# Five instead of eight transfers outstanding on SyncE's queue, in a fused attention and gated-linear-unit kernel

## The chip, the cores and the metric

The kernel runs on one core of a Trainium2 chip. The core has five engines with instruction streams of their own: TensorE (PE, with its weight loads shown as PEld), VectorE (DVE), ScalarE (ACT), GpSimd (POOL) and SyncE (SP), and 16 DMA engines that move data between HBM and the on-chip memory. SyncE computes nothing here: it issues transfers. The metric is the time of one execution on the device, in microseconds (us).

## The reference

Blockwise causal attention over 8 batches, 8 heads, 576 positions and 64 features is followed by a gated linear unit whose gate comes from a causal convolution over five positions:

```python
def _attn_ref(q, k, v):
    block = 64
    scores = scale * np.matmul(q, k.transpose(0, 1, 3, 2))
    mask = block_i >= block_j          # by blocks of 64 positions
    scores = np.where(mask, scores, -1000000000.0)
    scores = scores - np.max(scores, axis=-1, keepdims=True)
    attn = np.exp(scores)
    attn = attn / (np.sum(attn, axis=-1, keepdims=True) + 1e-09)
    return np.matmul(attn, v)

def _moe_ref(x, w_val, conv_w, w_out):   # x: heads side by side, (8, 576, 512)
    for k in range(5):
        gate_pre += conv_w[k] * xp[:, k:k + S, :]
    gate = 1.0 / (1.0 + np.exp(-gate_pre))
    return gate * (x @ w_val) @ w_out
```

All inputs and the output are float32.

## The kernel before

The order of all work is written out by hand: `PLAN` (lines 12 to 118) is a list of words such as `lv/9.0/S`, each an operation, its arguments, the engine and, for TensorE, the PSUM banks. A loop at the end of the kernel (line 677) calls the operations in that order, so each engine's instruction order is the order of its words. Semaphores between engines are put in by the framework, from what each instruction reads and writes.

The work is cut by heads. A unit u (16 of them) is four heads, half a batch; a pair p (32 of them) is two heads. For each unit, q and k are loaded in two halves each (`lq`, `lk`, line 272, 288 KB a half) into the float32 tiles `qs` and `ks`, of which there are three each. A cast to float16 (`cd`) goes into `qk16`, TensorE transposes it (`Tt`), a copy (`Te`) brings it into `qkT`, and TensorE makes the scores (`S`), ScalarE the exponentials (`E`). For each pair, v is loaded in two halves (`lv`, line 285, 128 KB each) into `vs`, five tiles, and cast (`cv`) into `v16`; the last 64 positions of v of a whole batch come separately (`lvt`, line 291, tile `vts`, cast `cvt`, used by the products `AT`). The products with v (`A`) are normalized and transposed into `xt`. Over runs of 464 positions follow the convolution (`C`), its gate (`CS`), the value product (`V`) and the gating (`Ve`), and then, per 128 rows, the output product (`O`), its copy (`Oe`) to one of six tiles `osb`, and the store (`Od`, line 649, 256 KB). The two weight matrices come in two transfers each (`lwv` line 296, `lwo` line 301) and the convolution's weights in one (`lcv` line 306). Most casts are made by GpSimd, some by VectorE and ScalarE. In the first microseconds TensorE also runs products on a zero tile (`w0`).

All transfers but two are issued by SyncE, one after the other, in the order of the list. Only `OLd` (line 662), the two last stores of 128 KB, is issued by ScalarE. A transfer waits at SyncE until its buffer is free, or, for a store, until its data is there; while it waits, the transfers behind it in the list wait too. Each transfer reports its landing on one of eight semaphores, taken in turn. The transfer eight places later uses the same semaphore and waits for that landing before it is issued, so at most eight are outstanding at a time. The choice of the engine is this dictionary, and a transfer is issued like this:

```python
    DMA = {"S": nc.sync, "A": nc.scalar}
...
        DMA[eng].dma_start(out=rot(qks[i], u)[0:128, h], in_=x)
```

Of the kernel before, what the change touches and what calls it, by code (L numbers as in the profile page):

```python
# [121 lines left out]
def kernel(  # L122
# [16 lines left out]
    B, H, SEQ, D = q.shape  # L139
# [20 lines left out]
    def consts(n, shape, dt, tag):  # L160
        return [const(shape, dt, f"{tag}_{i}") for i in range(n)]
# [52 lines left out]
    olast = [late[0:128, 256 * i:256 * i + 256] for i in range(2)]  # L214
    conv_nat = late[0:5, 0:512]

    qks = [consts(3, [128, 2, 576], fp32, f"{n}s") for n in "qk"]
    vs = consts(5, [128, 4, 2, 64], fp32, "vs")
    vts = consts(2, [128, 8, 64], fp32, "vts")
# [14 lines left out]
    w_val_st = gv[0:128, 0:4096].bitcast(fp32).rearrange("p (f n) -> p f n", f=4)  # L234
    gv = gv.rearrange("p (f s) -> p f s", f=4)
    osb_all = const([128, 6 * 512], fp32, "osb")
    osb = [osb_all[0:128, 512 * i:512 * i + 512] for i in range(6)]
    w_out_st = osb_all[0:128, 0:2048].rearrange("p (f n) -> p f n", f=4)
# [5 lines left out]
    def rot(tiles, i):  # L244
        return tiles[i % len(tiles)]

    DMA = {"S": nc.sync, "A": nc.scalar}

    def copy(eng, out, in_):
        if eng == "A":  # L250
            i = nc.scalar.copy(out=out, in_=in_)  # L251
        else:
            i = (nc.vector if eng == "V" else nc.gpsimd).tensor_copy(out=out, in_=in_)  # L253
        made.append(i)
# [10 lines left out]
    def load_qk(i, u, h, eng):  # L265
        b, w = divmod(u, 2)
        x = (q, k)[i][b]
        if u in ALONE:
            x = x[4 * w + 2 * h:4 * w + 2 * h + 2].rearrange("y (p n) d -> (y p) (n d)", n=9)
        else:  # L270
            x = x[4 * w + h:4 * w + h + 3:2].rearrange("x (p n) d -> p x (n d)", n=9)
        DMA[eng].dma_start(out=rot(qks[i], u)[0:128, h], in_=x)  # L272

    @op
    def lq(u, h, eng="S", bank=None):
        load_qk(0, u, h, eng)

    @op
    def lk(u, h, eng="S", bank=None):
        load_qk(1, u, h, eng)  # L280

    @op
    def lv(p, h, eng="S", bank=None):
        b, g = divmod(p, 4)
        DMA[eng].dma_start(
            out=rot(vs, p)[0:128, 0:4, h, 0:64],
            in_=v[b, 2 * g + h, 0:512, 0:64].rearrange("(c p) d -> p c d", p=128))

    @op
    def lvt(b, eng="S", bank=None):  # L290
        DMA[eng].dma_start(out=vts[b % 2][0:64, 0:8, 0:64],
                           in_=v[b, 0:8, 512:576, 0:64].rearrange("h s d -> s h d"))

    @op
    def lwv(f, eng="S", bank=None):
        DMA[eng].dma_start(out=w_val_st[0:128, 2 * f:2 * f + 2],
                           in_=moe_w_val[256 * f:256 * f + 256].rearrange("(f p) n -> p f n", p=128))

    @op
    def lwo(f, eng="S", bank=None):  # L300
        DMA[eng].dma_start(out=w_out_st[0:128, 2 * f:2 * f + 2],
                           in_=moe_w_out[256 * f:256 * f + 256].rearrange("(f p) n -> p f n", p=128))

    @op
    def lcv(eng="S", bank=None):
        DMA[eng].dma_start(out=conv_nat[0:5, 0:512], in_=moe_conv_w[:, :])


    @op
# [325 lines left out]
    def rows(u, t):  # L635
        return out2d[1152 * u + 128 * t:1152 * u + 128 * t + 128]
# [9 lines left out]

    @op
    def Od(u, t, eng, bank=None):
        DMA[eng].dma_start(out=rows(u, t), in_=rot(osb, 9 * u + t)[0:128])

    @op
    def OL(i, eng, bank):
# [6 lines left out]

    @op  # L660
    def OLd(i, eng, bank=None):
        DMA[eng].dma_start(out=rows(B // 2 - 1, 8)[:, 256 * i:256 * i + 256], in_=olast[i][0:128])

    nc.vector.memset(wz[0:128], 0.0)
    nc.vector.memset(tiny[0:128], 0.0)  # L665
# [11 lines left out]
    for word in PLAN.split():  # L677
        name, args, eng, bank = (word.split("/") + [""])[0:4]
        a = [int(i) for i in args.split(".") if i]
# [51 lines left out]
```

## Time and profile before

| | |
|---|---|
| time, median of 3 runs | 176.22 us (175.95 to 177.16) |
| the profiled execution: time | 175.31 us |
| the profiled execution: span of the instructions | 173.5 us |
| mean granted TensorE clock | 0.997 |
| DMA | 40.37 MB, 53693 packets, mean 233 GB/s |
| HBM | 30.42 MB read, 9.44 MB written |

All times inside the kernel are counted from the start of the span. In the rows of the profile, a line begins with the kernel's line, the engine and the operation, then what it writes and reads, as in `vs<-in_v_dram` for a load of v. SPq is the sequencer of SyncE, where transfers are issued. A row of transfers gives their count, the size of one and the median time from issue to landing; a row with min/median/max in front of its times gives the three of them for a group. A row of waits names who waited for whom, the total in us, how often, and the longest. A row of the order of time gives start, duration, the instruction, and in brackets the idle time of the engine before it and what ended it. The engine groups that take most time are the products of TensorE (line 146), ScalarE's exponentials (line 424, 93.4 us) and VectorE's copies out of PSUM (line 253). Line 253 is the shared helper of copies and casts.

### The profile page before, as it was taken

What the parts mean: (1) busy time and instruction counts of PE and PEld (TensorE: products, weight loads), DVE (VectorE), ACT (ScalarE), POOL (GpSimd) and SP (SyncE); (2) the same over time, 40 slices, a digit from 0 to 9 for tenths busy, and PEclk for the clock granted to TensorE, in tenths of its full rate; (3) what the DMA queues carried; (4) which work ended last, traced back from release to release, by engine and by line L of the source; (5) the groups of instructions that cost most, each with busy time, mean ns of one, the idle gap of its engine ahead of it and who ended that gap; (6) DMA issues with size and microseconds to landing.
All of it is one profiled execution on the core that took longest, in us unless ns stands there. A gap on an engine that the chain in (4) does not pass through costs nothing.

```text
span 173.5 us, 7920 instructions
## 1 busy us (share of the span) xinstructions
PE 165.5 (95%) x3397; PEld 96.6 (56%) x3397; DVE 127.5 (73%) x256; ACT 138.0 (80%) x162; POOL 72.2 (42%) x144
## 2 busy tenths in 40 slices
PE   7889999999999999999999999999999999999991
PEld 2335566457554865675445657484656565665440
DVE  4377998389968889799339879998699895645420
ACT  4589999789958989988987785898989768853641
POOL 5222836846367763671356418160466112100000
PEclk9999999999999999999999999999999999999998
DMA  5999899999999998999988999899688010302565
GB/s 170 333 380 259 198 302 384 331 191 279 253 215 280 245 186 258 298 337 333 289 253 244 333 252 261 253 311 243 148 289 268 7 62 2 117 14 95 192 231 212
DMA packets 53693, 40.37 MB, mean 233 GB/s; under 512 B 39701, under 2 KB 39957, under 8 KB 53658
## 3 DMA queue, kind: packets, MB, share of 16 engines
q1 hardware_dynamic: 53370, 39.61, 78.0%
q8 instruction: 26, 0.43, 1.0%
q10 hardware_dynamic: 288, 0.26, 0.4%
q14 instruction: 9, 0.07, 0.2%
HBM read 30.42 MB, written 9.44 MB: 230 GB/s over the span
## 4 chain that ended last, share of the span: by engine, by line
PE 77%; DVE 11%; issue 4%; DMA 3%; ACT 2%; SPq 1%; POOL 0%; DVEq 0%; POOLq 0%
PE PS L146 70%; PE PS L150 7%; DVE qkT L253 5%; DMA ks<-in_k_dram 3%; DVE gv L624 2%; ACT pt L424 1%; DVE x L494 1%; DVE xt L253 1%; DVE v L253 1%; DVE rc L489 1%; SPq L272 0%; POOL k L253 0%; DVE DG L570 0%; ACT xt L251 0%; DVE late L253 0%
## 5 line engine op out<-in xcount | busy, mean ns | idle before, releaser
L424 ACT ACTIVATE pt<-PS 128x1024 f16<-128x1024 f32 x96 | 93.4, 1027 | 11.9 <-PE PS L146 10.8
L253 DVE COPY qkT<-PS 128x1152 f16<-128x1152 f16 (+1 forms) x27 | 34.7, 1287 | 10.2 <-PE PS L150 9.2
L624 DVE SCALAR_TENSOR_TENSOR gv<-th,PS 128x112 f16<-128x112 f32 (+5 forms) x64 | 25.8, 448 | 16.1 <-PE PS L146 8.5
L146 PE MATMUL PS<-w_out,gv 128*128 128x512 f16 (+1 forms) x148 | 35.7, 374 | 0.3
L146 PE MATMUL PS<-xt,w_val 128*128 128x464 f16 x160 | 35.8, 360 | 0.1
L146 PE MATMUL PS<-qkT 64*128 64x64 f16 (+4 forms) x384 | 34.5, 276 | 0.6 <-DVE qkT L253 0.5
L146 PEld LDWEIGHTS <-pt 128*128 128x128 f16 (+1 forms) x960 | 28.0, 102 | 7.6 <-issue 2.8
L146 PE MATMUL PS<-v,pt 128*128 128x65 f16 (+1 forms) x896 | 30.7, 194 | 0.5 <-DVE rc L489 0.4
L606 ACT ACTIVATE th<-PS 128x928 f32<-128x928 f32 x20 | 18.0, 945 | 8.2 <-PE PS L146 8.2
L460 POOL MEMSET pt<- 64x256 f16 x32 | 10.1, 319 | 33.8 <-ACT pt L424 31.3
L494 DVE TENSOR_TENSOR x<-PS,rc 128x512 f16<-128x512 f32 x32 | 22.1, 690 | 0.9
L146 PEld LDWEIGHTS <-w_val 128*128 128x128 f16 x160 | 14.0, 98 | 14.6 <-issue 3.0
L253 POOL CAST k<-ks 128x1152 f16<-128x1152 f32 (+1 forms) x15 | 16.8, 1121 | 11.3 <-DMA ks<-in_k_dram 7.8
L146 PEld LDWEIGHTS <-qkT 64*128 64x128 f16 x384 | 13.3, 94 | 14.6 <-issue 12.2
L146 PEld LDWEIGHTS <-gv 128*128 128x128 f16 x148 | 12.8, 98 | 14.4 <-issue 3.2
L465 POOL MEMSET pt<- 64x256 f16 x32 | 10.2, 320 | 18.3 <-ACT pt L424 17.5
L253 POOL CAST q<-qs 128x1152 f16<-128x1152 f32 x12 | 13.7, 1148 | 3.9 <-DMA qs<-in_q_dram 2.9
L146 PE MATMUL PS<-xt,DG 32*32 32x464 f16 x800 | 13.9, 359 | 1.0 <-issue 0.8
L253 POOL CAST v<-vs 128x512 f16<-128x512 f32 x19 | 12.2, 640 | 5.9 <-DMA vs<-in_v_dram 4.5
L146 PE MATMUL PS<-th 128*128 128x512 f16 x41 | 13.0, 438 | 1.2 <-DVE tiny L665 1.2
L253 DVE COPY osb<-PS 128x512 f32<-128x512 f32 x18 | 12.2, 684 | 1.6 <-PE PS L146 1.6
L251 ACT COPY osb<-PS 128x512 f32<-128x512 f32 x17 | 10.0, 591 | 4.2 <-PE PS L146 4.2
(58 smaller groups left out, 136.0 us busy)
## 6 DMA issues: line engine op xcount, KB each, us to landing
qs<-in_q_dram SPq DMA_DIRECT2D x32, 288.0 KB, 5.1
ks<-in_k_dram SPq DMA_DIRECT2D x32, 288.0 KB, 5.0
out_dram<-osb SPq DMA_DIRECT2D x35, 256.0 KB, 3.7
vs<-in_v_dram SPq DMA_DIRECT2D x64, 128.0 KB, 4.6
gv<-in_moe_w_val_dram SPq DMA_DIRECT2D x2, 512.0 KB, 5.1
vts<-in_v_dram SPq DMA_DIRECT2D x8, 128.0 KB, 4.7
osb<-in_moe_w_out_dram SPq DMA_DIRECT2D x2, 512.0 KB, 6.9
out_dram<-late ACTq DMA_DIRECT2D x2, 128.0 KB, 2.1
```

Of the source, the lines that this page charges most:

```text
L146: made.append(nc.tensor.matmul(out=out, lhsT=lhsT, rhs=rhs, start=start, stop=stop, skip_group_check=True))
L150: made.append(nc.tensor.transpose(out=out, in_=in_, identity=identity))
L251: i = nc.scalar.copy(out=out, in_=in_)
L253: i = (nc.vector if eng == "V" else nc.gpsimd).tensor_copy(out=out, in_=in_)
L424: made.append(nc.scalar.activation(out=o, in_=r, func=AF.Exp, bias=0.0, scale=0.125))
L460: nc.gpsimd.memset(rot(pts, p)[64:128, 0:2, 0:1152].rearrange("p h (t s) -> p h t s", t=2)[:, :, :, 0:64], 0.0)
L465: nc.gpsimd.memset(rot(pts, p)[64:128, 0:2, 1024:1408].rearrange("p h (t s) -> p h t s", t=2)[:, :, :, 0:64], 0.0)
L489: made.append(nc.vector.reciprocal(out=rot(rcs, p)[0:128], in_=r[:, :, :, 64:65]))
L494: made.append(nc.vector.tensor_tensor(out=rot(x16, p)[0:128].rearrange("p i h d -> p h i d"), in0=r[:, :, :, 0:64], in1=rot(rcs, p)[0:128] ...
L606: made.append(nc.scalar.activation(out=rot(ths, n)[0:128, 2 * i:2 * i + 2], in_=both(take("C", n, i))[:, :, 0:RUN], func=AF.Tanh, bias=0.0 ...
L624: made.append(nc.vector.scalar_tensor_tensor(out=gv[0:128, x, a - 4 * i:e - 4 * i], in0=rot(ths, n)[0:128, x, a - o:e - o], scalar=1.0, in ...
```

## The change

Every transfer is now issued through a function `move`. For SyncE's transfers it keeps the list of those issued so far, and adds to each, from the sixth on, a dependency on the one five places ahead in SyncE's order. The dependency is of the kind that stands for data, so that it asks for the landing. ScalarE's two transfers go through the same function and get no dependency. Order, sizes, tiles and all other work stay as they were.

```diff
     DMA = {"S": nc.sync, "A": nc.scalar}
+    AHEAD, moved = 5, []
+    landed = mybir.DependencyInfo(mybir.DependencyClass.Sync, mybir.DependencyReason.DATA)
+
+    def move(eng, out, in_):
+        i = DMA[eng].dma_start(out=out, in_=in_)
+        if eng == "S":
+            if len(moved) >= AHEAD:
+                tc.add_manual_dep(i.ins, moved[-AHEAD].ins.name, landed, reason="few transfers at a time")
+            moved.append(i)
...
-        DMA[eng].dma_start(out=rot(qks[i], u)[0:128, h], in_=x)
+        move(eng, out=rot(qks[i], u)[0:128, h], in_=x)
...
-        DMA[eng].dma_start(out=rows(u, t), in_=rot(osb, 9 * u + t)[0:128])
+        move(eng, out=rows(u, t), in_=rot(osb, 9 * u + t)[0:128])
```

The other issuing lines (`lv`, `lvt`, `lwv`, `lwo`, `lcv`, `OLd`) are changed in the same way.

More of the change, by code (lines that the diff above doesn't have):

```diff
@@ L284, in lv @@
         b, g = divmod(p, 4)
-        DMA[eng].dma_start(
+        move(eng,
             out=rot(vs, p)[0:128, 0:4, h, 0:64],
@@ L290, in lvt @@
     def lvt(b, eng="S", bank=None):
-        DMA[eng].dma_start(out=vts[b % 2][0:64, 0:8, 0:64],
+        move(eng, out=vts[b % 2][0:64, 0:8, 0:64],
                            in_=v[b, 0:8, 512:576, 0:64].rearrange("h s d -> s h d"))
@@ L295, in lwv @@
     def lwv(f, eng="S", bank=None):
-        DMA[eng].dma_start(out=w_val_st[0:128, 2 * f:2 * f + 2],
+        move(eng, out=w_val_st[0:128, 2 * f:2 * f + 2],
                            in_=moe_w_val[256 * f:256 * f + 256].rearrange("(f p) n -> p f n", p=128))
@@ L300, in lwo @@
     def lwo(f, eng="S", bank=None):
-        DMA[eng].dma_start(out=w_out_st[0:128, 2 * f:2 * f + 2],
+        move(eng, out=w_out_st[0:128, 2 * f:2 * f + 2],
                            in_=moe_w_out[256 * f:256 * f + 256].rearrange("(f p) n -> p f n", p=128))
@@ L305, in lcv @@
     def lcv(eng="S", bank=None):
-        DMA[eng].dma_start(out=conv_nat[0:5, 0:512], in_=moe_conv_w[:, :])
+        move(eng, out=conv_nat[0:5, 0:512], in_=moe_conv_w[:, :])
     @op
@@ L661, in OLd @@
     def OLd(i, eng, bank=None):
-        DMA[eng].dma_start(out=rows(B // 2 - 1, 8)[:, 256 * i:256 * i + 256], in_=olast[i][0:128])
+        move(eng, out=rows(B // 2 - 1, 8)[:, 256 * i:256 * i + 256], in_=olast[i][0:128])
     nc.vector.memset(wz[0:128], 0.0)
```

## The prediction

> **What bounds the kernel now.** I read the page first, for the span and the chain of waits.
>
> ```profile
> span 173.5 us, 7920 instructions
> PE 165.5 (95%) x3397; PEld 96.6 (56%) x3397; DVE 127.5 (73%) x256; ACT 138.0 (80%) x162; POOL 72.2 (42%) x144
> ...
> PE 77%; DVE 11%; issue 4%; DMA 3%; ACT 2%; SPq 1%; POOL 0%; DVEq 0%; POOLq 0%
> PE PS L146 70%; PE PS L150 7%; DVE qkT L253 5%; DMA ks<-in_k_dram 3%; DVE gv L624 2%; ACT pt L424 1%; DVE x L494 1%; DVE xt L253 1%; DVE v L253 1%; DVE rc L489 1%; SPq L272 0%; POOL k L253 0%; DVE DG L570 0%; ACT xt L251 0%; DVE late L253 0%
> ```
>
> TensorE carries the end: 95% busy, 77% of the chain. Transfers hold 3% of it, one kind of load. So the change can act only by making a load late enough for TensorE to stand still. Where that can happen, the busy time by stretch and the waits of GpSimd show; GpSimd makes most of the casts that stand between a load and TensorE.
>
> ```profile
> core 0: us, PE busy (x) PEld busy (x) DVE busy (x) ACT busy (x) POOL busy (x), PEclk, DMA share, GB/s
> 0.00:70.00 70.00, 65.73 (x1369) 37.59 (x1369) 54.39 (x103) 59.08 (x68) 37.97 (x83) 1.00 0.95 267
> 70.00:132.00 62.00, 61.85 (x1352) 37.34 (x1348) 49.86 (x103) 53.00 (x61) 30.15 (x50) 1.00 0.94 275
> ```
> ```profile
> POOL k L253 <- DMA ks<-in_k_dram: 7.8, 4, 3.6
> POOL v L253 <- DMA vs<-in_v_dram: 4.5, 5, 1.7
> POOL v16t L253 <- DMA vts<-in_v_dram: 3.0, 2, 2.5
> POOL q L253 <- DMA qs<-in_q_dram: 2.9, 2, 2.4
> ```
>
> Nearly all idle time of TensorE before 132 us lies in the first 70: 70 - 65.73 = 4.3 us, against 0.15 us from 70 to 132. All that while the DMA engines are 94 to 95% busy, and GpSimd waits 7.8 + 4.5 + 3.0 + 2.9 = 18.2 us for loads. The load stream is thus a second resource near its limit, hidden behind TensorE with little to spare in the first half. The question is what a limit of five does to it.
>
> **How many are outstanding today.** The page lists the transfers with their time to landing; the last row is that list for 140 to 175 us alone.
>
> ```profile
> qs<-in_q_dram SPq DMA_DIRECT2D x32, 288.0 KB, 5.1
> ks<-in_k_dram SPq DMA_DIRECT2D x32, 288.0 KB, 5.0
> out_dram<-osb SPq DMA_DIRECT2D x35, 256.0 KB, 3.7
> vs<-in_v_dram SPq DMA_DIRECT2D x64, 128.0 KB, 4.6
> gv<-in_moe_w_val_dram SPq DMA_DIRECT2D x2, 512.0 KB, 5.1
> vts<-in_v_dram SPq DMA_DIRECT2D x8, 128.0 KB, 4.7
> osb<-in_moe_w_out_dram SPq DMA_DIRECT2D x2, 512.0 KB, 6.9
> ...
> late<-in_moe_conv_w_dram SPq DMA_DIRECT2D x1, 10.0 KB
> ```
> ```profile
> out_dram<-osb SPq DMA_DIRECT2D x14, 256.0 KB, 2.2
> ```
>
> SyncE issues 32 + 32 + 35 + 64 + 2 + 8 + 2 + 1 = 176 transfers. Without the 14 late stores, 162 go out in the first 132 us: one every 0.81 us. With about 4.9 us from issue to landing, 4.9 / 0.81 = 6 are outstanding on average. Eight is then seldom reached, and SyncE's waits for landings bear that out:
>
> ```profile
> SPq L285 <- DMA qs<-in_q_dram: 0.8, 3, 0.4
> SPq L272 <- DMA osb<-in_moe_w_out_dram: 0.7, 1, 0.7
> SPq L285 <- DMA osb<-in_moe_w_out_dram: 0.7, 1, 0.7
> SPq L272 <- DMA qs<-in_q_dram: 0.3, 1, 0.3
> ```
>
> Together 0.8 + 0.7 + 0.7 + 0.3 = 2.5 us. So today's limit costs almost nothing, while five lies below the mean of six: the new wait will bind at most of these 162 transfers, where the old one bound at six.
>
> **The change, part by part.** It removes no transfer and moves none in the order; it adds a wait ahead of each from the sixth on. Queued behind a waiting issue on SyncE is only the rest of the same list, loads and stores; no compute is issued there. The two stores that ScalarE issues at the very end are untouched.
>
> *The wait instruction.* The wait for the eighth before becomes empty, since each is implied by the waits of three transfers earlier, so about as many waits stand as before. A separate one is 17 ns.
>
> ```profile
> L285 SPq DMA_DIRECT2D vs<-in_v_dram x64: 379/507/2525, 10.6 to 131.6; - x64
> L285 SPq EVENT_SEMAPHORE  x21: 17/17/17, 30.9 to 130.3; - x21
> ```
>
> Even 17 ns on all 162 is 2.8 us spread over a queue that has 0.81 us per transfer and needs 0.51 us for one issue: 0 on the path, covered by that 0.3 us of room. If the cover were gone it would be those 2.8 us.
>
> *Steady flow.* Five outstanding give five landings per time to landing. What that time falls to when little is queued shows in the shortest ones (first a row for v, then q and k, then stores), and for v in a sparse stretch, 118 to 124 us:
>
> ```profile
> DMA to landing us min/median/max: 2.4/4.6/8.1
> ```
> ```profile
> DMA to landing us min/median/max: 3.0/5.1/8.1
> ```
> ```profile
> DMA to landing us min/median/max: 2.0/3.7/6.3
> ```
> ```profile
> vs<-in_v_dram SPq DMA_DIRECT2D x6, 128.0 KB, 2.9
> ```
>
> Five per 2.4 to 3.0 us is one per 0.48 to 0.60 us, against the 0.81 us that the stream needs. Even at 2.9 us for v it is 0.58 us, the rate at which SyncE issues them anyway (0.51 us and a gap). The other 2 us of today's 4.6 to 5.1 us is time spent queued, and a queue does not make the engines faster. So in steady flow landings stay where they are: 0 us. I weigh one rule here. The Trainium skill (DMA: Bandwidth & Descriptors, Latency and other measured facts) says that the latency of HBM rises from 0.2 us to 2 us under high load, and that lighter load makes a transfer's fixed cost smaller. By that rule five outstanding could land sooner than the queue alone explains, which would make the term negative; that is the third rival. No run here separates queueing from latency yet.
>
> *Breaks in the flow.* A deeper queue is worth something only when SyncE is held up. That happens when an instruction fetch occupies a DMA engine (queue 8), and the issue beside it takes long. The rows: the fetches of the whole run, those of 0 to 75 us, one long issue.
>
> ```profile
> q8 instruction: 26, 0.43, 1.0%
> ```
> ```profile
> q8 instruction: 11, 0.18, 1.0%
> ```
> ```profile
> 65.99 2.12 SPq L272 DMA_DIRECT2D qs<-in_q_dram  x1
> ```
>
> One fetch takes 1.0% x 16 x 173.5 / 26 = 1.07 us of one engine. It holds the stream by about that much with eight or with five, so only the difference counts. Where one is issuing, that issue lasts up to 2.1 to 2.5 us, so up to 2 us longer. The engines' own pace with a full queue, from 6 to 12 us (nearly all q and k) and from 42 to 50 us (mostly v):
>
> ```profile
> DMA packets 1079, 2.21 MB, mean 369 GB/s; under 512 B 118, under 2 KB 118, under 8 KB 1079
> ```
> ```profile
> DMA packets 4471, 2.04 MB, mean 254 GB/s; under 512 B 4024, under 2 KB 4024, under 8 KB 4469
> ```
>
> That is 288 KB in 0.80 us and 128 KB in 0.52 us. With five, four transfers are queued behind the landed one: 2.1 us of work for v, 3.2 us for q and k, and 1.1 us more while the fetch holds. A newcomer needs its shortest time less its own service, 2.4 - 0.5 = 1.9 us or 3.0 - 0.8 = 2.2 us, plus the up to 2 us of a long issue. For q and k that is 4.2 against 4.3 us: covered. For v it is 3.9 against 3.2 us: 0.7 us of empty engines at worst. Per fetch the cost is then 0 to 0.7 us; below zero it could go only if long issues were themselves caused by a long queue, which the third rival takes up. I take 0.15 us, near the lower end, since the median issue is 0.51 us and only v's runs fall short.
>
> *What a late load costs.* The tightest place that I find late enough for losses to have added up is the cast of v's tail at 61.5 us, which waits for its load, and the group of products that reads it. Next is a cast of k that TensorE turns at once.
>
> ```profile
> 61.52 0.62 POOL L253 CAST v16t<-vts 128x512 f16<-128x512 f32 x1 [0.57 <-DMA vts<-in_v_dram]
> ```
> ```profile
> 62.71 0.25 PE L146 MATMUL PS<-v,pt 128*64 128x65 f16 x4
> ```
> ```profile
> 72.56 1.15 POOL L253 CAST k<-ks 128x1152 f16<-128x1152 f32 x1 [0.36 <-PE PS L146]
> ```
> ```profile
> 74.13 0.43 PE L150 MATMUL PS<-ident,k 64*128 64x64 f16 x18
> ```
>
> The first cast ends at 62.14, 0.57 us before TensorE needs it; the second at 73.71, 0.42 us before. About 9 of the 11 fetches up to 75 us lie ahead of 61.5 (11 x 61.5 / 75). Their loss adds up in the queue: 9 x 0.15 = 1.35 us, less 0.57 of slack, makes TensorE 0.8 us later. Once TensorE has shifted, the later loads have that much more time, so shifts do not add: the end moves by the largest one. The stores of the tail wait for their data, not for five landings: 14 in 32 us, each landed in 2.2 us.
>
> **The sum.** 0 (wait instructions) + 0 (steady flow) + 1.35 - 0.57 = +0.8 us on a span of 173.5 us. The profiled execution took 175.3 us, 1.8 us more than its span; it becomes 176.1. The median of the runs, 176.22 us, lies 0.9 above it, so I forecast 177.0 us, +0.4%. Ends of the unknown term: 0 and 9 x 0.7 - 0.57 = +5.7 us, so 176.2 to 181.9 us.
>
> **Rivals.** *The stream starves* (slower). The place is the runs of v loads with a fetch in them, 42 to 62 us; the price is a loss per fetch nearer to 0.7 us. At 0.5 us it is 9 x 0.5 - 0.57 = +3.9 us, 180.1 us. It decides from (1.76 + 0.57) / 9 = 0.26 us per fetch, above which the kernel is over 1% slower. For it speaks that the engines are 95% busy and have no time to give back, against it the 0.2 to 0.3 us per transfer that five leave over.
>
> *The wait does not bite.* If the added dependency asked only for the issue, or were folded into an existing wait, nothing would change: 176.2 us. Against it stands that the six outstanding leave no way for a true wait to stay unseen.
>
> *Relief* (faster). Shorter queues shorten the long issues or the latency, loads land sooner, and TensorE's idle time before 70 us shrinks. All of it is 4.3 us; half of it gives 174.1 us. For it: SyncE's longest issues, 2.5 us among v's 64, are five times the median. Against it: the chain of the page holds loads of k alone, 3% of the span, so most late casts delay nothing that ends last. The Trainium skill's rule on latency under load, above, would lead here.
>
> **How the numbers follow.** Hidden but for about 1 us: 0.52, of which a fifth passes 1% (about what a measurement of this kernel can tell from no change). Starved: 0.28. Does not bite: 0.08. Relief: 0.12, three quarters of it beyond 1%. Slower by over 1%: 0.10 + 0.28 = 0.38. Within: 0.42 + 0.08 + 0.03 = 0.53. Faster: 0.09. For the range I leave out the relief beyond half a per cent and the upper third of the starved case: 175.3 to 181.0 us; the likeliest case alone has 176.2 to 178.2.
>
> **What would show it.** Right: SyncE waits for landings at most issues up to 132 us, the median time to landing falls from 4.6 to 5.1 us to about 4, the DMA share before 70 us stays near 0.95, the cast of v's tail starts 1 to 2 us after 61.5, and TensorE's busy time is the same while its idle time grows by about 0.8 us, all before 85 us. Starved: the DMA share falls below 0.9 and GpSimd waits well over 18 us for loads. No bite: SyncE's waits as before. Relief: fewer issues over 1 us, casts earlier than now. A shift that arises after 132 us would contradict all of it, for there the limit binds nothing.

## The result and the profile after

The changed kernel takes 186.51 us (median of 4 runs, 184.86 to 187.18), against 176.69 us (175.95 to 177.98) for the kernel before on the same chip: a ratio of 1.0571, with a 95% interval of 1.0517 to 1.0626. The prediction had 177.0 us with a range of 175.3 to 181.0. The profiled execution took 186.54 us with a span of 184.7 us, 11.2 us more than before. One variant further down, with the limit in the second half alone, scattered by almost 4% from execution to execution, and its ratio counts its three undisturbed executions alone, below the median of all ten.

The page of the changed kernel: span, TensorE, its granted clock in tenths over 40 slices, the DMA queue that SyncE feeds, and the chain of waits by engine and by line.

```profile
span 184.7 us, 7920 instructions
...
PE 168.0 (91%) x3397; PEld 97.8 (53%) x3397; DVE 127.6 (69%) x256; ACT 138.8 (75%) x162; POOL 72.2 (39%) x144
...
PEclk9999996699999999999999999999999999999999
...
q1 hardware_dynamic: 53370, 39.61, 73.3%
...
PE 46%; DMA 29%; DVE 10%; issue 5%; SPq 4%; ACT 2%; POOL 1%; DVEq 0%; POOLq 0%; ACTq 0%
PE PS L146 42%; DMA ks<-in_k_dram 9%; DMA vs<-in_v_dram 8%; DMA out_dram<-osb 8%; DMA qs<-in_q_dram 4%; SPq L252 4%; PE PS L150 4%; DVE gv L633 2%; DVE x L503 2%; DVE qkT L262 2%; ACT pt L433 1%; DVE osb L262 1%; DVE xt L262 1%; DVE rc L498 1%; DVE v16t L262 1%
```

TensorE's busy time is nearly that of before (168.0 against 165.5 us; part of the difference is the slices at half clock), and the span is 11.2 us longer: TensorE stands still. The chain has gone from 3% to 29% of transfers, now of k, v, q and stores alike. The share of the DMA queue fell, from 78.0 to 73.3%: the same bytes in more time.

Busy time by stretch: busy us and instruction counts of each engine, granted clock, DMA share, GB/s.

```profile
core 0: us, PE busy (x) PEld busy (x) DVE busy (x) ACT busy (x) POOL busy (x), PEclk, DMA share, GB/s
0.00:70.00 70.00, 63.86 (x1299) 36.80 (x1300) 51.48 (x97) 56.47 (x64) 36.90 (x82) 0.95 0.88 249
70.00:132.00 62.00, 57.94 (x1314) 34.50 (x1289) 44.74 (x92) 50.02 (x57) 25.38 (x43) 1.00 0.85 246
20.00:30.00 10.00, 7.53 (x164) 4.95 (x163) 7.31 (x14) 8.45 (x9) 4.46 (x10) 0.94 0.88 262
30.00:40.00 10.00, 10.00 (x194) 4.86 (x190) 5.26 (x11) 6.55 (x7) 6.70 (x10) 0.72 0.96 284
```

In the first 70 us TensorE is idle for 70 - 63.86 = 6.1 us, against 4.3 before; from 70 to 132 us for 62 - 57.94 = 4.1 us, against 0.15. The DMA engines were 94 to 95% busy in both stretches; now it is 88 and 85%. The granted clock, 1.00 in every stretch of before up to 132 us, is 0.94 and 0.72 between 20 and 40 us.

What SyncE and GpSimd wait for (who waits for whom: total us, times, longest us).

```profile
SPq L252 <- DMA qs<-in_q_dram: 14.8, 25, 1.4
...
SPq L252 <- DMA ks<-in_k_dram: 9.6, 26, 0.9
...
SPq L252 <- DMA vs<-in_v_dram: 7.9, 11, 1.4
...
SPq L252 <- DMA out_dram<-osb: 3.5, 10, 1.0
SPq L252 <- DMA vts<-in_v_dram: 3.0, 5, 1.1
```

```profile
POOL k L262 <- DMA ks<-in_k_dram: 14.0, 6, 6.2
POOL q L262 <- DMA qs<-in_q_dram: 7.4, 4, 3.8
POOL v16t L262 <- DMA vts<-in_v_dram: 6.1, 3, 4.0
POOL v L262 <- DMA vs<-in_v_dram: 5.9, 5, 2.3
POOL q L262 <- DMA vs<-in_v_dram: 5.4, 1, 5.4
```

SyncE's waits for landings were 2.5 us at six transfers; these five rows hold 14.8 + 9.6 + 7.9 + 3.5 + 3.0 = 38.8 us at 25 + 26 + 11 + 10 + 5 = 77 of them: the limit binds. GpSimd's waits for loads grew from 18.2 us to 14.0 + 7.4 + 6.1 + 5.9 + 5.4 = 38.8. Times to landing fell by 0.3 to 0.7 us only:

```profile
qs<-in_q_dram SPq DMA_DIRECT2D x32, 288.0 KB, 4.6
ks<-in_k_dram SPq DMA_DIRECT2D x32, 288.0 KB, 4.4
out_dram<-osb SPq DMA_DIRECT2D x35, 256.0 KB, 3.4
vs<-in_v_dram SPq DMA_DIRECT2D x64, 128.0 KB, 3.9
```

Seen from the stream: the 162nd transfer of SyncE, the last one before the tail of stores, landed at 135.25 us before and at 149.04 us after, 13.8 us later. One goes out every 0.889 us, where it was 0.817.

The first place where it reaches TensorE, in order of time (start, duration, instruction, idle time before it and what ended that), with the cast that TensorE waits for:

```profile
27.12 0.32 PE L146 MATMUL PS<-v,pt 128*64 128x65 f16 x8
29.63 0.26 PE L146 MATMUL PS<-v16t,pt 128*64 128x65 f16 x2 [2.19 <-POOL v16t L262]
```

```profile
28.96 0.62 POOL L262 CAST v16t<-vts 128x512 f16<-128x512 f32 x1 [3.97 <-DMA vts<-in_v_dram]
```

The cast of the first tail of v started at 26.36 us before; now it starts at 28.96, after 3.97 us of waiting for its load, and TensorE stands still for 2.19 us. From 28.84 us, within that stop, its granted clock is 0.5 for 6.8 us. Comparing each product's start with the same one before (at the times of before), TensorE is 2.2 us late at 27 us, 3.8 at 33, 3.4 from 50 to 69, 4.3 to 4.8 between 71 and 106 us, and then loses again: 6.5 at 116, 8.0 at 123, 9.7 at 130 and 11.1 at 139, which is what the end shows.

### The profile page after: what moved, and what is told of

It is laid out like the page before. It is cut to its first block, busy times and chain, and to the rows that moved or that the text cites. A ratio compares the mean times of both kernels' runs of the same rounds, so it can differ in the third digit from the quotient of the medians.

```text
span 184.7 us, 7920 instructions
## 1 busy us (share of the span) xinstructions
PE 168.0 (91%) x3397; PEld 97.8 (53%) x3397; DVE 127.6 (69%) x256; ACT 138.8 (75%) x162; POOL 72.2 (39%) x144
## 3 DMA queue, kind: packets, MB, share of 16 engines
q1 hardware_dynamic: 53370, 39.61, 73.3%
## 4 chain that ended last, share of the span: by engine, by line
PE 46%; DMA 29%; DVE 10%; issue 5%; SPq 4%; ACT 2%; POOL 1%; DVEq 0%; POOLq 0%; ACTq 0%
PE PS L146 42%; DMA ks<-in_k_dram 9%; DMA vs<-in_v_dram 8%; DMA out_dram<-osb 8%; DMA qs<-in_q_dram 4%; SPq L252 4%; PE PS L150 4%; DVE gv L633 2%; DVE x L503 2%; DVE qkT L262 2%; ACT pt L433 1%; DVE osb L262 1%; DVE xt L262 1%; DVE rc L498 1%; DVE v16t L262 1%
## 5 line engine op out<-in xcount | busy, mean ns | idle before, releaser
L146 PE MATMUL PS<-qkT 64*128 64x64 f16 (+4 forms) x384 | 35.6, 280 | 1.5 <-DVE qkT L262 1.3
L146 PEld LDWEIGHTS <-pt 128*128 128x128 f16 (+1 forms) x960 | 28.8, 103 | 13.9 <-issue 7.8
L146 PE MATMUL PS<-v,pt 128*128 128x65 f16 (+1 forms) x896 | 31.5, 195 | 4.5 <-DVE osb L262 1.5
L474 POOL MEMSET pt<- 64x256 f16 x32 | 10.3, 323 | 17.2 <-ACT pt L433 16.5
L146 PE MATMUL PS<-xt,DG 32*32 32x464 f16 x800 | 13.8, 380 | 0.0
```

What stands on the lines that cost most here:

```text
L146: made.append(nc.tensor.matmul(out=out, lhsT=lhsT, rhs=rhs, start=start, stop=stop, skip_group_check=True))
L474: nc.gpsimd.memset(rot(pts, p)[64:128, 0:2, 1024:1408].rearrange("p h (t s) -> p h t s", t=2)[:, :, :, 0:64], 0.0)
```

## The experiments

Three theories were told apart. Theory 1 is the prediction's own picture: the limit costs something only at breaks, where an instruction fetch of TensorE holds up the stream. Theory 2: five are too few in any flow. Theory 3, formed after the first runs: the loss stands where a half of q or k follows little queued work. In many of the runs only the transfers are left of the program; each of these was executed once.

### The transfers alone, with eight and with five, without and with fetches

All these kernels keep the transfers, their order and their tiles, zero the output tiles first, and leave out everything else; two of them add products on the zero tile so that TensorE's instructions are fetched. With eight, the added dependency is off.

```diff
-            if len(moved) >= AHEAD:
+            if False:
...
-    for word in PLAN.split():
+    only = [w for w in PLAN.split() if w.split("/")[2] == "S" or w.startswith("OLd")]
+    only = [w for x in only for w in (x, "w1//P/0")]     # the two with products alone
+    for word in only:
```

> All compute is left out: SyncE issues the same 176 transfers in the same order from and to the same tiles, at most eight outstanding, and TensorE has no instructions, so that hardly an instruction fetch (queue 8) falls into the stream. This is the base of a pair. If the breaks beside fetches are what eight costs today, the last transfer lands near the sum of the services, 176 transfers at about 0.6 us = 110 us, with no gap between landings over 0.4 us beyond a transfer's service. If gaps come from something else in the stream, they stay.

> The same transfers alone, five outstanding. Theory 1 (the limit costs only at breaks beside an instruction fetch): within 2 us of the same kernel with eight. Theory 2 (five cannot keep the engines full even in steady flow, as the time to landing does not fall with fewer outstanding): 8 to 10% longer, about 10 us, as the stream of the changed kernel was against the one before (0.89 against 0.82 us per transfer).

> The same transfers alone, eight outstanding, with a run of products of a zero tile on TensorE (13 after each word of the list, 128x64) that touch no loaded data, so that TensorE's instructions are fetched all the while. The time of the kernel is TensorE's; what counts is when the last of the first 162 transfers lands. Theory 1: later than without TensorE's instructions by about 1.2 us for each fetch inside the stream. Theory 2 and any other without fetches: the same as without them.

> As before with five outstanding. Theory 1: the stream is longer than with eight by 0.4 to 0.7 us for each fetch inside it, as between the two full kernels (13.8 us over 23 fetches, 0.6 us each). Theory 2: longer by the same 10 us as in the pair without TensorE's instructions.

The pages of the transfers alone, first with eight, then with five (span; packets, MB and share of 16 engines of SyncE's queue, which passes 100% because at times more than 16 packets are under way):

```profile
span 132.4 us, 234 instructions
...
q1 hardware_dynamic: 53370, 39.61, 104.7%
```

```profile
span 149.0 us, 236 instructions
...
q1 hardware_dynamic: 53370, 39.61, 92.6%
```

Five cost 149.0 - 132.4 = 16.6 us with no product and no fetch in the program, and the 162nd landing comes at 138.8 instead of 122.6 us. Theory 1 falls, and the loss is larger than Theory 2's 10 us. With eight, too, the stream is longer than the 110 us expected of the services alone, so its gaps do not come from fetches only. With products and their fetches the two take 144.6 and 156.6 us of span, and the 162nd lands at 134.6 and 146.6: a loss of 12.0 us, less than without. For 18 fetches that is 0.67 us each, which by itself would have fitted Theory 1's 0.4 to 0.7; only the pair without fetches shows that they are not the cause. Products and fetches together slow the stream, but with eight more than with five.

Compared landing by landing, 12.7 of the 15.3 us that five lose after the eleventh transfer stand at q and k, 2.6 us at v and stores together. Within q and k the loss was 0.57 us each where the four transfers ahead held under 700 KB, 0.30 between 700 and 900 KB and 0.10 above. That led to Theory 3. In the whole kernel the same comparison comes out otherwise: of the 12.6 us after the eleventh transfer 11.8 stand at v, 1.3 at q and k and -0.5 at the rest. There transfers also wait for tiles and for data; why the loss stands at v stays open.

### Who has to wait

One variant lets only q and k wait for the fifth before, the other only all the rest; the limit of eight stays for those that are free. Each was run as transfers alone and as the whole kernel.

```diff
-            if len(moved) >= AHEAD:
+            if len(moved) >= AHEAD and big:      # "and not big" in the other
...
-        move(eng, out=rot(qks[i], u)[0:128, h], in_=x)
+        move(eng, out=rot(qks[i], u)[0:128, h], in_=x, big=True)
```

> The transfers alone, without compute; only the 64 q and k transfers wait for the fifth before them, all others as with eight. In the pair with eight and five for all, landings lost 15.3 us, of which 12.7 us stood at q and k transfers (0.57 us each where the four ahead carry under 700 KB, 0.30 from 700 to 900, 0.10 above). Theory 3 (a q or k transfer that is issued with too few KB queued ahead of it finds the engines empty before its own data flow): close to five for all, transfer 162 lands at 133 to 138 us against 122.6 with eight and 138.8 with five. Theory 2 (five are too few for any kind): about in proportion to the 64 of 162, 129 us.

> The transfers alone, the other way round: all but the q and k transfers wait for the fifth before them. Theory 3: most of the loss is gone, transfer 162 lands at 123 to 127 us. Theory 2: 132 us, the larger part of the loss, as 98 of the 162 wait.

The transfers alone: the 162nd landing at 136.0 us where q and k wait (13.4 of the 16.2 us lost) and at 134.2 us where the others wait (11.6 of 16.2). Theory 3 had expected 133 to 138 for the first, which fits, and 123 to 127 for the second, which misses. In both, most of the loss stands at q and k (11.6 of 13.3 us and 10.2 of 11.4 us after the eleventh). SyncE issues in order: a v that is held holds the q behind it, so both variants shorten the queue that a q or k meets.

> The full kernel, only q and k transfers wait for the fifth before them. Theory 3: most of the 5.7% stays, ratio 1.035 to 1.057. Theory 2: 1.02 to 1.03.

> The full kernel, all but the q and k transfers wait for the fifth before them. Theory 3: ratio 1.00 to 1.015, and no half clock of TensorE at 29 us. Theory 2: 1.03 to 1.04.

In the whole kernel the first has a ratio of 1.0348 (1.0283 to 1.0412), at the lower end of what Theory 3 expected (1.035 to 1.057) and above Theory 2's 1.02 to 1.03. The second took 177.91, 181.84, 180.75 and 183.90 us, too scattered for a ratio; its profiled execution, of 177.91 us, has no stop of TensorE at 27 us and no half clock, as Theory 3 expected. Neither is as slow as all of them waiting. The wait of q and k alone costs time; whether that of v and stores alone does in the kernel is not settled.

### Grouped by kind, and the limit from four to eight

To take the mixture of sizes away, the same transfers alone were grouped: weights, all q and k, all v, all stores.

```diff
+    group = {"lcv": 0, "lwv": 0, "lwo": 0, "lq": 1, "lk": 1, "lv": 2, "lvt": 2, "Od": 3, "OLd": 4}
+    only.sort(key=lambda w: group[w.split("/")[0]])
```

> The transfers alone, with the limit of eight, grouped by kind: the five of the weights, then all halves of q and k in the plan's order, then all of v and its tails, then the stores of six fixed tiles, then the two last stores; compute is left out, so the output is not the reference's. It serves as the mate of the next run. In the plan's order the 176 took a span of 132.4 us with eight. Both theories expect 128 to 136 us here.

> The same grouped transfers with the limit of five; compute is left out. In the plan's order five cost 149.0 - 132.4 = 16.6 us of span. Theory 2 (five are too few in any flow, since one comes to its landing only some 4 us after its issue): q and k then move at one per 4.4 / 5 = 0.88 us instead of about 0.80, v at one per 3.4 / 5 = 0.68 instead of 0.50, so the loss stays at 12 to 18 us and stands with v, too. Theory 3 (the loss stands where a large q or k follows little queued work, that is four transfers with less than 900 KB in them): among q and k there are always four halves, 1152 KB, ahead, so their part loses under 2 us; v's part (four of 128 KB ahead) loses little, because each is small; the whole loss is under 5 us.

> The grouped transfers with a limit of six; compute is left out. Measured so far: a half of q or k lands 3.06 us after its issue when alone, one comes every 0.755 us with eight and every 0.924 us with five; v at 0.67 and stores at 0.68 us are the same with both. By the time alone, 3.06 / 0.755 = 4.05, so that from five on the limit should cost nothing at all. If instead engines that run dry between two packets are the loss (no packet of q or k over 250 ns with eight, 3.7% of them with five), a sixth gives each engine 0.75 us more of work: q and k fall back to 0.75 to 0.80 us, the span to 136.5 to 139 us, and the share of long packets below 1%. If a slower state of the chip made the run with five, six stays near 0.9.

> The grouped transfers with a limit of four; compute is left out. By the time alone, q and k are then at (3.06 + 0.02) / 4 = 0.77 us each, hardly slower than with eight, v at 2.2 / 4 = 0.55, which is under the 0.67 measured. By dry engines the queue ahead holds 2.3 us of work against the 2.3 us that a new transfer takes before its own service, so that every small delay leaves some engine dry: 1.0 to 1.2 us each for q and k, and the span 153 to 165 us; v starts to lose, too.

From the pages with eight and with five, the span and the time to landing of q and v:

```profile
span 136.5 us, 244 instructions
...
qs<-in_q_dram SPq DMA_DIRECT2D x32, 288.0 KB, 6.0
...
vs<-in_v_dram SPq DMA_DIRECT2D x64, 128.0 KB, 4.0
```

```profile
span 147.1 us, 237 instructions
...
qs<-in_q_dram SPq DMA_DIRECT2D x32, 288.0 KB, 4.7
...
vs<-in_v_dram SPq DMA_DIRECT2D x64, 128.0 KB, 3.1
```

From the landings and the packet records of the traces (a half of q or k is 128 packets of 2304 bytes, which take 93 to 95 ns in the median):

```
limit   span    q,k: us between landings   packets over 250 ns of 8192 (their mean)   v: us   stores: us
  8     136.5          0.755                     0                                    0.672    0.679
  6     139.0          0.796                    83  (530 ns)                          0.665    0.680
  5     147.1          0.924                   288  (484 ns)                          0.673    0.677
  4     158.6          1.040                   369  (463 ns)                          0.727    0.682
```

The loss of five is 64 x (0.924 - 0.755) = 10.8 us, all of the 147.1 - 136.5 = 10.6 us. It stands in a pure run of q and k with 1152 KB always ahead, where Theory 3 expected under 2 us; and v and stores lose nothing, where Theory 2 expected v to lose too. Each was half right: five are too few for q and k in any order (10.6 of the 16.6 us of span), the mixed order adds some 6, and v and stores by themselves need no more than five. With six the pace is nearly back, as the account of engines that run dry had it (0.75 to 0.80 expected; its share of long packets, under 1%, came out at 83 / 8192 = 1.0%). With four that account held for q and k (1.040, expected 1.0 to 1.2), where the time of a lone transfer gave 0.77.

Two rivals can be set aside. The issue of a q or k takes 0.54 us in the median with every one of the four limits, so SyncE did not become slower. Nor was the whole execution slow: v and stores of the run with five keep their pace.

The packet records also tell how many packets are under way at each moment. During the run of q and k with eight it is never fewer than 16, as many as there are engines. With six it is fewer for 14% of the time, with five for 47% (down to 8), with four for 64% (down to 2): then some engine must stand empty while others work. With five the missing packets come to 3.3 us per engine, and the 288 long ones to 288 x (484 - 93) ns / 16 = 7.0 us: together 10.3 of the 10.8 us lost. Empty moments alone are not yet a loss: in v's run they grow from 17 to 42% of the time with five, and v keeps its pace.

### One at a time

```diff
-    AHEAD, moved = 5, []
+    AHEAD, moved = 1, []
```

> The transfers alone in the plan's order, each issued when the one before it has landed; compute is left out. It measures what the prediction took from the shortest rows: the time from issue to landing of a transfer with nothing else on the engines. By the prediction's rows it is 3.0 us for a half of q or k, 2.4 for v, 2.0 for a store, and the span 64 x 3.0 + 72 x 2.4 + 35 x 2.0 + 5 = some 450 us with the gaps of issue. If instead the shortest rows were of transfers that met a lucky moment, the medians are 3.5 us and more, and the bound of the prediction was wrong at its root: then five outstanding could not carry one per 0.8 us even in theory.

The page's list of transfers (count, size, median us to landing):

```profile
span 448.1 us, 237 instructions
...
qs<-in_q_dram SPq DMA_DIRECT2D x32, 288.0 KB, 3.1
ks<-in_k_dram SPq DMA_DIRECT2D x32, 288.0 KB, 3.1
out_dram<-osb SPq DMA_DIRECT2D x35, 256.0 KB, 2.0
vs<-in_v_dram SPq DMA_DIRECT2D x64, 128.0 KB, 2.2
```

The prediction's bounds from the shortest rows (3.0, 2.4 and 2.0 us) were right: alone, it is 3.1, 2.2 and 2.0 us, and the span of 448.1 us is what they give. Of the 8192 packets of q and k, 646 took over 250 ns here, 404 ns in the mean; all begin within 1.04 us of their transfer's first packet, nine in ten within 0.44 us. So an engine that has nothing queued pays some 0.3 us more (404 - 93 ns) on a packet of q or k when it starts. With eight in a pure run, no packet is like that. In the plan's order some are with eight, too: 170 of the 8192 in the transfers alone (392 with five) and 313 in the kernel before (426 in the changed one).

### In the kernel: which stretch, how many, and what stands behind it

Six instead of five; five only up to the 82nd transfer, or only from the 83rd on; and five with nine output tiles instead of six.

```diff
-    AHEAD, moved = 5, []
+    AHEAD, moved = 6, []                          # six
...
-            if len(moved) >= AHEAD:
+            if AHEAD <= len(moved) < 82:          # first_half
+            if len(moved) >= 82:                  # second_half
...
-    osb_all = const([128, 6 * 512], fp32, "osb")
+    osb_all = const([128, 9 * 512], fp32, "osb")  # nine_out_tiles, and the list of tiles made from it
```

> Six outstanding, nothing else changed. If the loss is the depth that is lacking at each break, one transfer more (0.5 to 0.75 us of queued work) covers most of the 0.6 us that five lose per fetch: under 3 us slower than the kernel before, ratio 1.00 to 1.017. If five is slow in steady flow, six is too, by about the share 5/6 of the loss: ratio about 1.03.

> Five outstanding for the transfers 6 to 82 (up to the k load that is cast at 72.6 us in the kernel before), eight after that. TensorE was 4.6 us late at that place in the changed kernel, from a late v load at 27 us and a half clock after it. If nothing is added later, the end moves by that: ratio 1.02 to 1.03. The rest of the 5.7% belongs to the second half.

> Eight outstanding up to transfer 82, five from there. My first account (only loads can hold TensorE, and after 75 us they have 4 to 20 us to spare): no change, ratio 1.00 to 1.005. The new account (late stores keep the six output tiles occupied, and the products wait for a free one from 106 us on): 3 to 6 us slower, ratio 1.02 to 1.035, with VectorE waiting for stores to land.

> Five outstanding everywhere, nine output tiles in place of six. If late stores that keep output tiles occupied cause the second part of the loss (6.5 us between 106 and 139 us), most of it goes: ratio 1.02 to 1.03, and no wait of VectorE for stores to land. If the late loads of the second half cause it, the ratio stays at 1.05 to 1.06.

Six: 178.11 us, ratio 1.0103 (1.0009 to 1.0197), as expected of a lack of depth (1.00 to 1.017) and not of a loss that shrinks by 5/6 only (about 1.03); the grouped run with six, too, loses 64 x (0.796 - 0.755) = 2.6 us and not 10.8. In the profiled execution the 162nd transfer lands at 140.6 us, 5.3 us later than with eight, of which 3.7 us reach the span; the clock stays at 1.0. The first half alone: 180.66 us, ratio 1.0257 (1.0164 to 1.0351), as expected (1.02 to 1.03); TensorE is 5.9 us late at 80 us and loses nothing afterwards. The second half alone: ratio 1.0104 (1.0023 to 1.0185), with executions from 176.43 to 183.07 us and 180.0 in the median of ten. That lies between the two expectations, no change (1.00 to 1.005) and 1.02 to 1.035. Its profile says little of the second half: TensorE is 2.7 us late at 75 us there, where the program is still that of the kernel before, so that executions differ by this much on their own. By the ratios the two halves make 3.6% together, both at once 5.7%. That the first half uses up the stream's lead, so that the second has none left to lose, would fit; it was not tested by itself.

The waits of TensorE in the first half's run show the same stop at 27 us; the half clock that begins within it lasts 3.4 us:

```profile
PE PS L146 <- POOL v16t L262: 2.1, 1, 2.1
```

Nine output tiles: 186.27 us (183.59 to 189.33), ratio 1.0568 (1.0399 to 1.0738); the 1.02 to 1.03 expected if the tiles were the cause lies outside. In the changed kernel VectorE waited 6.4 us for stores to free an output tile, and TensorE for VectorE's copies into these tiles, which looked like the cause of the losses after 106 us:

```profile
PE PS L146 <- DVE osb L262: 3.1, 3, 1.5
```

With nine both waits are gone, and GpSimd's waits for k, which were 14.0 us in the changed kernel, have grown:

```profile
POOL k L262 <- DMA ks<-in_k_dram: 17.7, 8, 6.6
```

So the output tiles are not the whole cause; the loads are late there too. A part for the tiles is not excluded: in the profiled execution with nine (183.59 us, the fastest) TensorE loses 3.1 us between 106 and 139 us, against 6.8 in the changed kernel.

### The half clock

Six products on the zero tile fill the stop at 27 us.

```diff
-AT/0/P/2 Nm/3/V
+w0/6.128.0/P/2 AT/0/P/2 Nm/3/V
```

> The changed kernel (limit of five) with six products on the zero tile ahead of the products of the first tail of v, where TensorE stood still for 2.2 us at 27 us and its granted clock was 0.5 for 6.8 us afterwards. If the half clock is a part of the loss by itself, it goes (clock 0.99 or more), and the time falls by 1 to 2 us, ratio 1.045 to 1.050. If the lateness of the loads alone sets the end, later loads take up what the clock gives back, and the ratio stays within 1.053 to 1.062.

```profile
span 180.8 us, 7932 instructions
...
PEclk9999999999999999999999999999999999999999
```

The clock is 1.0 throughout. The time is 184.04 us, ratio 1.0494 (1.0416 to 1.0571) against 1.0571 (1.0517 to 1.0626): in the middle it is the 1 to 2 us expected of the clock, but the intervals overlap, so the size stays unsettled. Most of the loss is there without the half clock.

No version with a lower limit beats the kernel before; six throughout (1.0103) and five in the second half alone (1.0104) are the nearest.

## Why the prediction was wrong, point by point

**What bounds the kernel.** Right: TensorE held the end, and a late load was the only way for the change to act. It also read rightly that the stream has little to spare, and that five would bind at most transfers.

**The wait instruction at 0.** Not contradicted: v and stores in the grouped runs keep their pace with five (0.673 against 0.672, 0.677 against 0.679 us), with the same waits in the list.

**Steady flow at 0: the step that failed.** The prediction divided the time of a lone transfer by five, 0.48 to 0.60 us, found it under the 0.81 us needed, and added that "a queue does not make the engines faster". The lone times were right, the inference from them was not. A pure run of q and k, with nothing else in the program, goes from 0.755 to 0.924 us each, while 3.06 / 5 = 0.61. What the runs showed in its place: with eight no packet of q or k is long and at least 16 are always under way; with five 3.5% take some 0.48 us instead of 0.09, as those do with which an idle engine starts, and for 47% of the time fewer than 16 are under way. A transfer has landed when the last of its packets has, so a few such packets delay the landing, and the landing five places back releases the next issue. Landings with five came 0.73 to 0.77 us apart for a while and then 1.2 to 1.8 us. The mean queue of 5 x 0.75 = 3.75 us against the 3.06 us of a lone transfer left 0.7 us of slack in the mean, and that was not enough to keep every one of the 16 engines fed. That some run dry while others work is shown by the count; the records do not say on which engine a packet ran, and why a first packet takes longer stays open. In the plan's order the term that was put at 0 is 16.2 us at the 162nd landing without compute, and 13.8 us in the kernel. From 10 us on up to that landing, the missing packets grow by 9.9 us per engine and the long ones by 6.4 without compute, in the kernel by 10.9 and 3.1; in the kernel an engine also stands empty when SyncE waits for a tile or for data, so there this is an account and no proof.

**Breaks in the flow at 9 x 0.15 us.** The mechanism was not what cost the time: the loss is larger without fetches (16.2 us) than with them (12.0 us). The split was the wrong way round for the grouped runs, too: q and k were called covered (4.2 against 4.3 us) and v short; there q and k lose and v does not. In the kernel the later landings do stand at v, for a reason that is open. What does hold is that products with their fetches slow the stream at either limit (below).

**The tightest place.** The prediction took the cast of v's tail at 61.5 us, since losses had to add up first. With a steady loss they add up sooner. The order of time of the kernel before, GpSimd and then TensorE, at the first tail:

```profile
26.36 0.62 POOL L253 CAST v16t<-vts 128x512 f16<-128x512 f32 x1 [2.47 <-DMA vts<-in_v_dram]
```

```profile
27.40 0.20 PE L146 MATMUL PS<-v16t,pt 128*64 128x65 f16 x2
```

That cast ended at 26.98, only 0.42 us ahead of the products that read it, and there TensorE lost its first 2.2 us, and more at half clock.

**"Shifts do not add: the end moves by the largest one."** Wrong for a stream that is slower throughout. TensorE was about 4.5 us late between 71 and 106 us and the load stream kept falling behind, so it lost another 6.6 us by 139 us. The stretch from 70 to 132 us, with 0.15 us of idle time before, has 4.1 now. The statement that nothing could arise after 85 us fell with it; 1.3 us arose after 132 us, which the prediction had named as contradicting all of it.

**The rivals.** "The stream starves" is what happened, with its sign and signs (DMA share below 0.9: 0.88 and 0.85; GpSimd waiting well over 18 us: 38.8), but at 180.1 us it was sized per fetch and in one stretch, and had a chance of 0.28. Relief did not show: TensorE's idle time before 70 us grew from 4.3 to 6.1 us. The Trainium skill (DMA: Bandwidth & Descriptors, Latency and other measured facts) says that lighter load makes the fixed cost smaller. The traces agree in direction alone: q lands in a median of 4.6 instead of 5.1 us in the kernel, 4.7 instead of 6.0 us in the grouped runs, and the pace got worse. These times hold the time queued as well, so the fixed cost by itself is not shown.

**What would show it.** Right were SyncE's waits at many issues (81 of the 157 that have a fifth before them) and, nearly, the median landing of about 4 us (3.9 to 4.6 us for v, k and q). Wrong were the DMA share "near 0.95", the cast of v's tail 1 to 2 us after 61.5 (it starts at 65.1) and TensorE's loss "all before 85 us".

## What to carry to other kernels

A limit on outstanding transfers is not judged by the time of a lone transfer divided by the limit. In these runs q and k of 288 KB, at 3.06 us alone and 0.755 us apiece, wanted more than six outstanding (4.5 us of work) to run at full pace, while transfers of 128 and 256 KB were content with five; to know it, run the transfers alone at two limits, without compute. Long packets alone do not tell, since the kernel before has 313 of them. In an in-order queue any held transfer shortens the queue of those behind it, and a loss in steady flow adds up from the start: look for the first tight consumer, not for the tightest late in the old trace.

## What the runs showed of the hardware

- **A packet after an empty engine is long.** Packets of 2304 bytes take 95 ns in the median and never over 250 in the pure run with eight, where at least 16 are always under way; when each transfer is alone, 646 of them, ten per transfer, take 404 ns in the mean, all near the transfer's start. None of v's packets of 256 bytes took over 204 ns in any of the runs.
- **Products with their instruction fetches cost the stream more than the fetches' own time.** With 18 fetches of 16 KB the 162nd landing moved from 122.6 to 134.6 us with eight outstanding, 0.67 us for each, though a fetch holds one of 16 engines for 1.17 us in the mean, 0.07 us shared by all. With five it was 138.8 to 146.6, 0.43 us for each. No run separates the fetches from the products themselves.
- **Half clock after a short stop.** TensorE's granted clock fell to 0.5 within stops of 2.1 to 2.4 us at 27 us, for 6.8 us in the changed kernel and 3.4 us in first_half and nine_out_tiles; with a stop of 1.7 us at the same place, where q and k alone wait, it stayed at 1.0. The Trainium skill (TensorE: Matmul & The Clock Gate, Part 1: The HAM clock gate) puts the window at about 3.4 us without work; here less than that was enough.
